# Another order for the last two units of a sliding-window attention and for wo's blocks

## The chip, the cores and the metric

The kernel runs on one core of a Trainium2 chip. The metric is the device time of one execution in microseconds (us), lower is better. Three runs of the kernel before took 217.32, 217.93 and 218.16 us; their median is 217.93 us.

## What is computed

One decoding step for two sequences (B = 2, one token each, D = 512), all in float32. `xn` is the layer norm of `x`. The output is `x + s * g`:

```python
q = (xn @ wq)                       # 32 heads of 128
k = k_cache[:, :, Sk - W:, :]       # the last W = 4096 of 32768 positions, 8 key heads
v = v_cache[:, :, Sk - W:, :]       # each key head serves 4 query heads
p = softmax(q k^T * 128 ** -0.5)
s = (p v).reshape(B, 1, 4096) @ wo  # wo is 4096 x 512: 8 MB
g = silu(gated_mlp(xn, w_in, w_sp, b_sp, w_out))
```

The windows of K and V are 2 x 8 x 4096 x 128 floats each, 32 MB apiece. With wq (8 MB), wo (8 MB) and the MLP's weights, 89.4 MB have to come from HBM, and each byte is used once.

## The kernel before

**Units and slots.** The 16 pairs of (sequence, key head) are handled two at a time, in eight units, 0 to 7. A unit's K and its V are one transfer of 4096 KB each. All large inputs go through a ring of four slots of 4096 KB (`ring`, line 105): the MLP's first weight, wq in two slots, then K and V in turn, and last wo in two slots, `wo0` and `wo1`. A transfer can be issued once the slot that it takes has been read for the last time. All of them are issued from SyncE's queue (SP) in program order.

**Steps of a unit.** VectorE turns K in eight pieces (`T:u.0` to `T:u.7`, line 373). For each half a of the unit TensorE multiplies the turned K with the queries (`shares`), ScalarE copies the product out of PSUM (`keep`), TensorE adds the shares up (`scores`), VectorE takes the maximum (`rowmax`). The maximum is shared (`mg`, `shmax`, `bias`), ScalarE takes the exponential (`exp`), VectorE turns the result (`probs_t`), and TensorE multiplies it with V (`pv`). The sum of the exponentials runs beside it (`lsum`, `shsum`, `weights`). At the end ScalarE moves the scaled result out of PSUM (`evac`), TensorE collects the heads (`col`), and VectorE adds them (`gather`).

**After a set of units.** The heads fall in three sets (`SETS`, line 360): the first holds half of wo's rows, the other two a quarter each. When the last unit of a set is gathered, TensorE spreads the heads (`spread:i`, line 490), VectorE places them as the stationary operand `oT` (`oT:i`, line 501), and the set's rows of wo can be multiplied. Set 0 is complete after unit 5, set 1 after unit 6, set 2 after unit 7.

**wo.** `wo0` holds set 0 (16 rows of 2 KB in each partition), `wo1` holds sets 1 and 2 (8 rows each). Line 515 cuts the loads: set 0 in two transfers of 2048 KB, set 1 in two of 1024 KB, set 2 in transfers of 1024, 512, 256 and 256 KB. So there are eight blocks. The steps `X` and `Y` (`wo_early`, line 523) multiply two rows each, for sets 0 and 1, into the PSUM tile `part`; twelve such steps make 24 multiplications. In code, `X:0.k` for k = 0 to 3 are block 0, for 4 to 7 block 1; `Y:0.0` and `Y:0.1` are block 2, `Y:0.2` and `Y:0.3` block 3.

**The end.** Lines 575 to 594 stand behind the order: ScalarE copies `part` to `parts`; TensorE multiplies blocks 4 to 7 (set 2) into `so`, with `parts` added after block 4; VectorE multiplies by the gate and adds x (`res`); SP stores 4 KB.

**Order.** The program order of all these steps is written out in the string `ORDER` (lines 27 to 52), and each engine's instructions are kept in it (`InOrder`, line 55). An engine works its own queue in that order: an instruction that waits holds up all that stand behind it on its engine, whatever they need themselves. Completion of transfers is signalled on eight semaphores that the framework gives to SP's transfers in turn, so a transfer also waits until the one eight places before it has landed.

Of the kernel before, what the change touches and what calls it, by code (L numbers as in the profile page):

```python
# [9 lines left out]
F32 = mybir.dt.float32  # L10
AF = mybir.ActivationFunctionType
# [3 lines left out]
P = 128  # L15
HQ, DH = 32, 128
G = 4
# [24 lines left out]
K:6 V:5 T:5.0 T:5.1 T:5.2 rowmax:4.1 mg:4 shmax:4 T:5.3 bias:4 shares:5.0 T:5.4 gather:3 exp:4.0 probs_t:4.0 T:5.5  # L42
T:5.6 exp:4.1 keep:5.0 pv:4.0 lsum:4 shsum:4 scores:5.0 T:5.7 shares:5.1 probs_t:4.1 pv:4.1 weights:4 keep:5.1
scores:5.1 evac:4 col:4 rowmax:5.0
K:7 V:6 T:6.0 rowmax:5.1 T:6.1 mg:5 T:6.2 shmax:5 T:6.3 T:6.4 bias:5 exp:5.0 exp:5.1 T:6.5 shares:6.0 probs_t:5.0
pv:5.0 lsum:5 T:6.6 keep:6.0 probs_t:5.1 T:6.7 shsum:5 scores:6.0 weights:5 shares:6.1 rowmax:6.0 pv:5.1
V:7 T:7.0 wo:0 keep:6.1 evac:5 scores:6.1 col:5 T:7.1 T:7.2 rowmax:6.1 mg:6 shmax:6 gather:5 spread:0 T:7.3 bias:6
T:7.4 T:7.5 shares:7.0 exp:6.0 probs_t:6.0 T:7.6 keep:7.0 pv:6.0 T:7.7 wo:1 exp:6.1 scores:7.0 shares:7.1 probs_t:6.1
keep:7.1 lsum:6 shsum:6 scores:7.1 rowmax:7.0 weights:6 pv:6.1 evac:6 rowmax:7.1 mg:7 shmax:7 col:6 oT:0 bias:7
gather:6 spread:1 exp:7.1 exp:7.0 probs_t:7.1 lsum:7 X:0.1 probs_t:7.0 X:0.3 X:0.2 shsum:7 weights:7 X:0.0 pv:7.0  # L50
pv:7.1 oT:1 evac:7 X:0.7 Y:0.1 X:0.4 X:0.5 col:7 Y:0.0 X:0.6 gather:7 spread:2 oT:2 Y:0.3 Y:0.2
"""


# [16 lines left out]
def kernel(  # L71
# [14 lines left out]
    pe, dve, act, sp = (InOrder(tc, e) for e in (nc.tensor, nc.vector, nc.scalar, nc.sync))  # L86
    B, _, D = x.shape
# [11 lines left out]
    DC = D // G  # L99
# [8 lines left out]
    sb = ctx.enter_context(tc.tile_pool(name="sb", bufs=2))  # L108
    ps = ctx.enter_context(tc.tile_pool(name="ps", bufs=1, space=bass.MemoryType.PSUM))

    def slot(name, *shape):
        return ring.tile([P, *shape], F32, tag="slot", name=name)

    def bank(name, *shape):
        return ps.tile([P, *shape], F32, tag="kt", name=name, bufs=2)
# [11 lines left out]
    for a in range(0, KT, 2):  # L127
        t = slot(f"wq{a}", 2, HQ * DH)
# [17 lines left out]
    def load(u, src, name):  # L146
        t = slot(f"{name}{u}", UJ, DH)
        b, v = divmod(u, HKV // 2)
        first = src[b, 2 * v, SK - W, :]
        of = bass.AP(tensor=src.tensor, offset=first.offset, ap=[[UJ * DH, P // 2], [SK * DH, 2], [1, UJ * DH]])  # L150
        sp.dma_start(t.rearrange("p j d -> p (j d)"), of)
        return t
# [17 lines left out]
    rowm = cst.tile([P, 32], F32, tag="rowm", name="rowm")  # L170
# [66 lines left out]
    for n in range(G):  # L237
        pz = bank(f"z{n}", 512)[:, :FC]
        for k in range(KT):
            pe.matmul(  # L240
                pz[32 * k : 32 * k + 32, :], xnT[:, k, :], win[:, k, n * FC : (n + 1) * FC],
                start=True, stop=True,
# [31 lines left out]
    u = cst.tile([P, 2, FT, B], F32, tag="u", name="u")  # L274
# [37 lines left out]
    for j in range(FT):  # L312
        for g in range(G):
            pe.matmul(
                y[32 * g : 32 * g + 32, :], hT[:, j, :], wout[:, j, g * DC : (g + 1) * DC],
                start=(j == 0), stop=(j == FT - 1),
# [20 lines left out]
    def place_queries():  # L337
        dve.tensor_tensor(
            free_ap(qb, 16, [[REP, G], [32, NP * G], [1, REP]]), free_ap(qa, 0, [[0, G], [REP, NP * G], [1, REP]]),
            free_ap(grpm, 0, [[1, G], [0, NP * G], [0, REP]]), op=ALU.mult,  # L340
        )

    gate = cst.tile([P, DC], F32, tag="gate", name="gate")

    def silu():
        dve.tensor_scalar(gate, ys, -1.0, 80.0, op0=ALU.mult, op1=ALU.min)
        act.activation(gate, gate, AF.Exp)
        dve.tensor_scalar_add(gate, gate, 1.0)
        dve.reciprocal(gate, gate)
        dve.tensor_mul(gate, gate, ys)  # L350
# [11 lines left out]
    for i, (kv, n, nj) in enumerate(SETS):  # L362
        o1 = cst.tile([P, B, 32], F32, tag=f"o1_{i}", name=f"o1_{i}")
        oT = cst.tile([P, nj, 32], F32, tag=f"oT_{i}", name=f"oT_{i}")
# [102 lines left out]
    col = {}  # L467
# [22 lines left out]
    def spread(i):  # L490
        o1, oT, nj = sets[f"oT{i}"]
        perm = {8: perm8, 16: perm16}[nj]
        nx = 32 // nj
        pts[i] = bank(f"oT_ps{i}", B, nj)
        for x in range(nx):
            pe.matmul(
                pts[i], perm[:, x].rearrange("p h a x -> p (h a x)"), o1[:, :, nj * x : nj * x + nj],
                start=(x == 0), stop=(x == nx - 1),
            )

    def place(i):
        dve.tensor_copy(sets[f"oT{i}"][1][:, :, 0 : 16 * B : 16], pts[i].rearrange("p b j -> p j b"))
# [6 lines left out]
    blocks = []  # L509

    def load_wo(n):
        t = slot(f"wo{n}", 16, D)
        a = 0
        for i in ((0,), (1, 2))[n]:
            for j, n in (((0, 8), (8, 8)), ((0, 4), (4, 4)), ((0, 4), (4, 2), (6, 1), (7, 1)))[i]:
                sp.dma_start(t[:, a : a + n, :], wo_s[i][:, j : j + n, :])
                blocks.append((t[:, a : a + n, :], sets[f"oT{i}"][1], j))
                a += n
# [4 lines left out]
    def wo_early(n, at):  # L523
        nonlocal done
        if done == 0:
            part.append(ps.tile([P, 512], F32, tag="s0", name="part"))
        t, oT, j = blocks[n]
        for a in range(at, at + 2):
            g = done % G
            pe.matmul(  # L530
                part[0][32 * g : 32 * g + 32, :], oT[:, j + a, :], t[:, a, :], start=(done < G), stop=(done >= EARLY - G)
            )
            done += 1

    part = []
    STEPS = dict(
        T=turn, rowmax=row_max, mg=spread_max, shmax=share_max, bias=bias, exp=probs, probs_t=probs_t, lsum=own_sum,
        shsum=share_sum, weights=weights, shares=shares, keep=keep, scores=scores, pv=pv, evac=evacuate, col=collect,
        gather=gather,
    )  # L540

    def step(name, u, a=()):
        if name == "q":
            place_queries()
        elif name == "silu":
            silu()
        elif name == "K":
            units[u].k = load(u, k_cache, "k")
        elif name == "V":
            units[u].v = load(u, v_cache, "v")  # L550
        elif name == "wo":
            load_wo(u)
        elif name == "spread":
            spread(u)
        elif name == "oT":
            place(u)
        elif name == "X":
            wo_early(a[0] // 4, 2 * (a[0] % 4))
        elif name == "Y":
            wo_early(2 + a[0] // 2, 2 * (a[0] % 2))  # L560
        else:
            STEPS[name](units[u], *a)

# [5 lines left out]
    for line in ORDER.strip().split("\n"):  # L569
        for name in line.split():  # L570
            name, at = name.split(":")
            u, _, a = at.partition(".")
            step(name, int(u), (int(a),) if a else ())

    parts = sb.tile([P, D], F32, tag="o", name="parts", bufs=1)
    act.activation(parts, part[0], AF.Copy)
    so = bank("so", DC)
    for n in range(4, len(blocks)):
        t, oT, j = blocks[n]
        for a in range(t.shape[1]):  # L580
            for g in range(G):
                pe.matmul(
                    so[32 * g : 32 * g + 32, :], oT[:, j + a, :], t[:, a, g * DC : (g + 1) * DC],
                    start=(j + a == 0), stop=(j + a == oT.shape[1] - 1),
                )
        if n == 4:
            for g in range(G):
                pe.matmul(
                    so[32 * g : 32 * g + 32, :], rowm, parts[:, g * DC : (g + 1) * DC], start=False, stop=False
                )  # L590
    res = cst.tile([P, DC], F32, tag="res", name="res")
    dve.tensor_mul(res, so, gate)
    dve.tensor_add(res, res, x4)
    sp.dma_start(bass.AP(tensor=out.tensor, offset=out.offset, ap=by_group), res[0 : P : P // (G * B), :])

# [27 lines left out]
```

## Time and profile before

| | before |
|---|---|
| runs shown (us) | 217.32, 217.93, 218.16 |
| profiled execution (us) | 217.48 |
| span from first to last instruction (us) | 215.7 |
| busy: PE, DVE, ACT (us) | 143.5, 126.3, 50.9 |
| mean granted TensorE clock | 0.826 |
| read from HBM | 89.40 MB, 414 GB/s over the span |

The profile is that of one execution; its own time of 217.48 us is its span of 215.7 us and 1.8 us around it. In its rows PE is TensorE's matmuls, PEld the loading of their stationary operand, DVE VectorE, ACT ScalarE and SPq SyncE's queue. Each operation stands as out<-in by the names of the tiles: `kts<-k` is `T`, `sh` is `shares`, `s` is `scores`, `p` is `exp`, `pT` is `probs_t`, `acc` is `pv`, `o<-acc` is `evac`, `col` is `col`, `o<-col` is `gather`, `oT_ps` is `spread`, `oT` is the placing, `part` is X and Y, and `so` is the last product. All lines appear as L65, since a helper there issues every instruction, so the tiles tell them apart. A float32 matmul leaves two records: the 24 multiplications of X and Y stand as 48.

### The profile page before, as it was taken

What the parts mean: (1) busy time and instruction counts of PE and PEld (TensorE: products, weight loads), DVE (VectorE), ACT (ScalarE), POOL (GpSimd) and SP (SyncE); (2) the same over time, 40 slices, a digit from 0 to 9 for tenths busy, and PEclk for the clock granted to TensorE, in tenths of its full rate; (3) what the DMA queues carried; (4) which work ended last, traced back from release to release, by engine and by line L of the source; (5) the groups of instructions that cost most, each with busy time, mean ns of one, the idle gap of its engine ahead of it and who ended that gap; (6) DMA issues with size and microseconds to landing.
All of it is one profiled execution on the core that took longest, in us unless ns stands there. A gap on an engine that the chain in (4) does not pass through costs nothing.

```text
span 215.7 us, 2477 instructions
## 1 busy us (share of the span) xinstructions
PE 143.5 (67%) x972; PEld 51.6 (24%) x972; DVE 126.3 (59%) x217; ACT 50.9 (24%) x128; POOL 5.2 (2%) x19
## 2 busy tenths in 40 slices
PE   0179694722864895954990796389168939975993
PEld 0128521300111232312220221122112322221342
DVE  2511212259598989849918972993698199534001
ACT  4111203200114236023330603142032305242020
POOL 8000000000000000000000000000000000000000
PEclk9998578785589699995796589579955985997999
DMA  6999999999999999999999999999999999999990
GB/s 256 426 438 444 407 428 468 395 463 407 462 413 441 431 425 444 419 448 407 456 413 456 419 441 431 419 444 422 450 409 462 407 450 419 441 401 428 419 376 23
DMA packets 4219, 89.56 MB, mean 415 GB/s; under 512 B 478, under 2 KB 494, under 8 KB 880
## 3 DMA queue, kind: packets, MB, share of 16 engines
q1 hardware_dynamic: 4188, 89.40, 96.6%
q8 instruction: 8, 0.13, 0.2%
q10 hardware_dynamic: 20, 0.01, 0.0%
q14 instruction: 3, 0.02, 0.0%
HBM read 89.40 MB, written 0.00 MB: 414 GB/s over the span
## 4 chain that ended last, share of the span: by engine, by line
DMA 57%; PE 20%; DVE 17%; ACT 4%; issue 1%; ACTq 0%
DMA k<-in_A_k_cache_dram 40%; DMA wo<-in_A_wo_dram 12%; DVE kts L65 11%; PE acc L65 7%; DMA win<-in_B_w_in_dram 5%; PE sh L65 5%; PE part L65 4%; ACT p L65 3%; PE s L65 3%; DVE pT L65 2%; DVE m L65 1%; PE so L65 1%; DVE gate L65 1%; DVE nb L65 1%; ACT ss L65 1%
## 5 line engine op out<-in xcount | busy, mean ns | idle before, releaser
L65 DVE STREAM_TRANSPOSE kts<-k 128x1024 f32<-128x1024 f32 x64 | 75.7, 1219 | 25.7 <-DMA k<-in_A_k_cache_dram 25.7
L65 PE MATMUL sh<-kts,qb 128*32 128x512 f32 x256 | 42.9, 793 | 12.5 <-DVE kts L65 9.0
L65 PE MATMUL acc<-v,pT 128*32 128x512 f32 x256 | 36.4, 676 | 6.9 <-DVE pT L65 4.0
L65 ACT ACTIVATE p<-s,nb 128x512 f32<-128x512 f32 x32 | 22.5, 730 | 38.6 <-DVE nb L65 38.6
L65 ACT ACTIVATE ss<-sh 128x512 f32<-128x512 f32 x16 | 9.6, 599 | 61.4 <-PE sh L65 61.4
L65 DVE STREAM_TRANSPOSE pT<-p 128x1024 f32<-128x1024 f32 x16 | 19.6, 1226 | 2.5 <-ACT p L65 2.5
L65 PE MATMUL s<-ss,sums 128*128 128x512 f32 x32 | 18.8, 671 | 2.1 <-ACT ss L65 2.1
L65 PE MATMUL mo<-mg,joint 128*128 128x16 f32 x16 | 4.2, 338 | 23.6 <-DVE mg L65 23.6
L65 PEld LDWEIGHTS acc<-v,pT 128*32 128x32 f32 x256 | 11.4, 143 | 32.6 <-issue 21.8
L65 PEld LDWEIGHTS sh<-kts,qb 128*32 128x32 f32 x256 | 8.8, 128 | 35.1 <-issue 31.1
L65 DVE TENSOR_REDUCE m<-s 128x1 f32<-128x512 f32 x16 | 10.8, 678 | 5.9 <-PE s L65 5.8
L65 PE MATMUL q_ps<-wq,xnT 128*32 128x512 f32 x64 | 11.0, 820 | 4.6 <-DMA wq<-in_A_wq_dram 4.6
L65 ACT ACTIVATE o<-acc,wd 128x128 f32<-128x128 f32 x32 | 9.1, 367 | 19.5 <-PE acc L65 19.5
L65 PE MATMUL part<-wo,oT 128*32 128x512 f32 x48 | 9.5, 709 | 2.4 <-DMA wo<-in_A_wo_dram 2.4
L65 PEld LDWEIGHTS mo<-mg,joint 128*128 128x128 f32 x16 | 3.3, 261 | 26.8 <-DVE mg L65 24.2
L65 PE MATMUL z<-win,xnT 128*32 128x448 f32 x32 | 5.2, 814 | 3.9 <-DMA win<-in_B_w_in_dram 3.9
L65 PEld LDWEIGHTS s<-ss,sums 128*128 128x128 f32 x32 | 5.0, 197 | 10.4 <-issue 7.4
L65 PE MATMUL zT_ps<-rowm,z 128*128 128x2 f32 x28 | 6.6, 370 | 0.0
L65 PEld LDWEIGHTS zT_ps<-rowm,z 128*128 128x128 f32 x28 | 6.5, 325 | 0.0
L65 ACT ACTIVATION_READ_ACCUMULATOR p<-s,nb 128x1 f32 x32 | 6.4, 200 | 0.0
L65 ACT ACT_TABLE_LOAD x4 | 5.1, 1283 | 2.6 <-POOL hT L164 2.6
L65 PE MATMUL xnT_ps<-ident,xn 2*128 2x2 f32 x4 | 0.6, 253 | 7.5 <-DVE xn L65 7.5
(108 smaller groups left out, 71.4 us busy)
## 6 DMA issues: line engine op xcount, KB each, us to landing
k<-in_A_k_cache_dram SPq DMA_DIRECT2D x8, 4096.0 KB, 23.8
v<-in_A_v_cache_dram SPq DMA_DIRECT2D x8, 4096.0 KB, 29.8
wq<-in_A_wq_dram SPq DMA_DIRECT2D x1, 4096.0 KB, 24.3
wq<-in_A_wq_dram SPq DMA_DIRECT2D x2, 2048.0 KB, 29.4
wo<-in_A_wo_dram SPq DMA_DIRECT2D x2, 2048.0 KB
win<-in_B_w_in_dram SPq DMA_DIRECT2D x1, 3584.0 KB
wo<-in_A_wo_dram SPq DMA_DIRECT2D x3, 1024.0 KB, 24.3
wout<-in_B_w_out_dram SPq DMA_DIRECT2D x1, 1792.0 KB, 15.0
```

Source lines behind the costliest of these rows:

```text
L65: return self.tc.keep_in_program_order(call(*args, **kwargs))
```

## The change

The string `ORDER` is another one from unit 6 on, set 0 and set 1 of wo come in one transfer each (4096 and 2048 KB, where there were two and two), and what stood behind the order is now part of it, as steps `Z` (one block of set 2 each), `parts` (the copy of `part`) and `pz` (adding it). `X:0.k` is now rows 2k and 2k + 1 of block 0, and `Y:0.k` the same of block 1: the same rows of wo as before. The loads of K and V keep their places in SP's queue. With three transfers fewer ahead of it, the store gets another of the eight semaphores.

Three things in the order are different. In units 5 to 7 the exponentials of both halves stand closer together and the sum's steps elsewhere among VectorE's turns. `pv:7.0` and `pv:7.1` now stand ahead of every X step, where X:0.1, X:0.3, X:0.2 and X:0.0 stood ahead of them. And spread:0 stands after unit 7's exponentials instead of in unit 7's turns.

```diff
-K:7 V:6 T:6.0 rowmax:5.1 T:6.1 mg:5 T:6.2 shmax:5 T:6.3 T:6.4 bias:5 exp:5.0 exp:5.1 T:6.5 shares:6.0 probs_t:5.0
-pv:5.0 lsum:5 T:6.6 keep:6.0 probs_t:5.1 T:6.7 shsum:5 scores:6.0 weights:5 shares:6.1 rowmax:6.0 pv:5.1
-V:7 T:7.0 wo:0 keep:6.1 evac:5 scores:6.1 col:5 T:7.1 T:7.2 rowmax:6.1 mg:6 shmax:6 gather:5 spread:0 T:7.3 bias:6
-T:7.4 T:7.5 shares:7.0 exp:6.0 probs_t:6.0 T:7.6 keep:7.0 pv:6.0 T:7.7 wo:1 exp:6.1 scores:7.0 shares:7.1 probs_t:6.1
-keep:7.1 lsum:6 shsum:6 scores:7.1 rowmax:7.0 weights:6 pv:6.1 evac:6 rowmax:7.1 mg:7 shmax:7 col:6 oT:0 bias:7
-gather:6 spread:1 exp:7.1 exp:7.0 probs_t:7.1 lsum:7 X:0.1 probs_t:7.0 X:0.3 X:0.2 shsum:7 weights:7 X:0.0 pv:7.0
-pv:7.1 oT:1 evac:7 X:0.7 Y:0.1 X:0.4 X:0.5 col:7 Y:0.0 X:0.6 gather:7 spread:2 oT:2 Y:0.3 Y:0.2
+K:7 V:6 T:6.0 rowmax:5.1 mg:5 T:6.1 T:6.2 shmax:5 bias:5 T:6.3 exp:5.0 T:6.4 exp:5.1 T:6.5 probs_t:5.0 shares:6.0
+keep:6.0 lsum:5 shsum:5 scores:6.0 probs_t:5.1 T:6.6 T:6.7 rowmax:6.0 pv:5.0 weights:5 shares:6.1 keep:6.1 pv:5.1
+V:7 T:7.0 wo:0 scores:6.1 rowmax:6.1 T:7.1 T:7.2 mg:6 T:7.3 shmax:6 bias:6 T:7.4 evac:5 col:5 exp:6.0 exp:6.1 T:7.5
+probs_t:6.0 T:7.6 T:7.7 wo:1 lsum:6 shares:7.0 keep:7.0 pv:6.0 scores:7.0 shares:7.1 rowmax:7.0 keep:7.1 shsum:6
+scores:7.1 probs_t:6.1 weights:6 rowmax:7.1 mg:7 pv:6.1 evac:6 shmax:7 gather:5 col:6 bias:7 exp:7.0 gather:6 exp:7.1
+probs_t:7.0 spread:0 probs_t:7.1 lsum:7 spread:1 pv:7.0 shsum:7 oT:0 weights:7 pv:7.1 X:0.6 X:0.0 oT:1 X:0.2 X:0.4
+evac:7 X:0.3 col:7 X:0.7 gather:7 spread:2 X:0.5 Y:0.1 Y:0.0 Y:0.3 X:0.1 Y:0.2 parts:0 oT:2 Z:0 Z:1 pz:0 Z:2 Z:3
...
-            for j, n in (((0, 8), (8, 8)), ((0, 4), (4, 4)), ((0, 4), (4, 2), (6, 1), (7, 1)))[i]:
+            for j, n in (((0, 16),), ((0, 8),), ((0, 4), (4, 2), (6, 1), (7, 1)))[i]:
...
+    def copy_parts():
+        parts.append(sb.tile([P, D], F32, tag="o", name="parts", bufs=1))
+        act.activation(parts[0], part[0], AF.Copy)
+
+    def wo_last(n):
+        if n == 0:
+            so.append(bank("so", DC))
+        t, oT, j = blocks[2 + n]
+        for a in range(t.shape[1]):
+            for g in range(G):
+                pe.matmul(
+                    so[0][32 * g : 32 * g + 32, :], oT[:, j + a, :], t[:, a, g * DC : (g + 1) * DC],
+                    start=(j + a == 0), stop=(j + a == oT.shape[1] - 1),
+                )
+
+    def add_parts():
+        for g in range(G):
+            pe.matmul(
+                so[0][32 * g : 32 * g + 32, :], rowm, parts[0][:, g * DC : (g + 1) * DC], start=False, stop=False
+            )
...
-            wo_early(a[0] // 4, 2 * (a[0] % 4))
+            wo_early(0, 2 * a[0])
         elif name == "Y":
-            wo_early(2 + a[0] // 2, 2 * (a[0] % 2))
+            wo_early(1, 2 * a[0])
+        elif name == "Z":
+            wo_last(u)
+        elif name == "parts":
+            copy_parts()
+        elif name == "pz":
+            add_parts()
...
-    parts = sb.tile([P, D], F32, tag="o", name="parts", bufs=1)
-    act.activation(parts, part[0], AF.Copy)
-    so = bank("so", DC)
-    for n in range(4, len(blocks)):
...
-    dve.tensor_mul(res, so, gate)
+    dve.tensor_mul(res, so[0], gate)
```

More of the change, by code (lines that the diff above doesn't have):

```diff
@@ L535 @@
     part = []
+    def copy_parts():
[16 more added lines that the diff above has]
+            )
+    parts, so = [], []
     STEPS = dict(
@@ L573 @@
             step(name, int(u), (int(a),) if a else ())
-    parts = sb.tile([P, D], F32, tag="o", name="parts", bufs=1)
-    act.activation(parts, part[0], AF.Copy)
-    so = bank("so", DC)
-    for n in range(4, len(blocks)):
[L579 to L590, printed above, removed]
     res = cst.tile([P, DC], F32, tag="res", name="res")
-    dve.tensor_mul(res, so, gate)
+    dve.tensor_mul(res, so[0], gate)
     dve.tensor_add(res, res, x4)
```

## The prediction, made before the changed kernel was run

> **What bounds the kernel now.** I read the page's queue line first, then the chain of waits in order of time, SP's rows, and last the tail by stretches.
>
> ```profile
> q1 hardware_dynamic: 4188, 89.40, 96.6%
> ```
> ```profile
> 89.05 25.00 DMA k<-in_A_k_cache_dram
> ...
> 126.12 26.71 DMA k<-in_A_k_cache_dram
> ...
> 171.43 25.47 DMA wo<-in_A_wo_dram
> ...
> 197.03 3.56 PE part L65 x12
> ...
> 210.10 2.12 PE so L65 x72
> ```
> ```profile
> 166.15 0.54 SPq L65 DMA_DIRECT2D v<-in_A_v_cache_dram  x1
> ```
> ```profile
> 171.43 0.81 SPq L65 DMA_DIRECT2D wo<-in_A_wo_dram  x2
> ```
> ```profile
> 184.01 2.23 SPq L65 DMA_DIRECT2D wo<-in_A_wo_dram  x5
> ```
> ```profile
> SPq L65 <- DVE res L65: 15.9, 1, 15.9
> SPq L65 <- DMA v<-in_A_v_cache_dram: 5.8, 1, 5.8
> SPq L65 <- DMA wo<-in_A_wo_dram: 4.5, 1, 4.5
> ```
> ```profile
> 192.07 0.33 SPq L65 DMA_DIRECT2D wo<-in_A_wo_dram  x1
> 212.89 0.69 SPq L65 DMA_DIRECT2D out_dram<-res  x1
> ```
>
> The transfers keep the 16 DMA engines at 96.6% of the span: one stream without a break. Its pace: K4 landed at 89.05 + 25.00 = 114.05 and K6 at 126.12 + 26.71 = 152.83, four transfers of 4096 KB later, so 9.70 us each. SP could issue the last piece of wo only at 192.07, when V7 had landed. The first half of set 0 landed at 171.43 + 25.47 = 196.90, so 2048 KB took 4.83 us. The other 6 MB of wo, at 9.70 us for 4 MB, end at 196.90 + 14.55 = 211.45.
>
> The stream never waits for a slot here: V7 was issued at 166.15, wo0 at 171.43, wo1 from 184.01 on, each with 16 to 20 us of earlier transfers still under way.
>
> The tail:
>
> ```profile
> 196.98:200.39 3.41, 3.36 (x12) 0.65 (x12) 0.00 (x0) 0.00 (x0) 0.00 (x0) 0.50 1.00 428
> 200.39:203.80 3.41, 3.41 (x32) 1.62 (x34) 0.48 (x3) 0.00 (x0) 0.00 (x0) 1.00 0.98 416
> 203.80:207.21 3.41, 3.41 (x40) 1.46 (x36) 0.00 (x0) 1.14 (x4) 0.00 (x0) 1.00 1.02 423
> ```
> ```profile
> 211.00:211.20 0.20, 0.20 (x12) 0.20 (x13) 0.00 (x0) 0.00 (x0) 0.00 (x0) 1.00 0.13 51
> 211.20:211.40 0.20, 0.20 (x16) 0.20 (x12) 0.00 (x0) 0.00 (x0) 0.00 (x0) 1.00 0.00 0
> ```
> ```profile
>   DMA wo<-in_A_wo_dram: 2.4, 1
> ```
> ```profile
> 210.23 0.60 ACT L65 ACTIVATE parts<-part 128x512 f32<-128x512 f32 x1 [3.67 <-PE part L65]
> 210.88 0.43 PE L65 MATMUL so<-parts,rowm 128*32 128x128 f32 x8
> 211.12 1.06 PE L65 MATMUL so<-wo,oT 128*32 128x128 f32 x32
> 212.24 0.29 DVE L65 TENSOR_TENSOR res<-so,gate 128x128 f32<-128x128 f32 x1 [2.85 <-PE so L65]
> ```
>
> The columns of the stretches are: length, busy time (and count) of PE, PEld, DVE, ACT and POOL, then granted clock, DMA share and GB/s. From 197.03 to 212.18 PE has no pause. It waits for wo exactly once, 2.4 us before 197.03: X:0.1 holds `pv:7.0` up in PE's queue until wo's first half is there. That wait costs twice, as the clock is 0.50 in the next stretch. The last bytes of wo leave the engines by 211.2, and my sum of landings says 211.45. So PE and the stream arrive together, PE perhaps a little later. **Two bounds of nearly the same height** make the end; moving PE's work can gain only what lies between them.
>
> **The change, part by part.**
>
> *Issues of V7, wo0 and wo1.* V7 waits for T:6.7, wo0 for `pv:5.1`, wo1 for T:7.7. VectorE does the same instructions between T:6.0 and T:6.7 as before, and up to T:7.7 one less (the gather of unit 5 comes later); TensorE does the same ones before `pv:5.1`. So each moves by less than 1 us, and the stream hides all of it; that cover of 16 us or more would have to go first. Cost: nothing. *Fewer transfers.* SP issues three less, and the last of wo need not wait for V7's landing, but the bytes ahead of it last until about 201.7 anyway: nothing. For size, 4 MB as two halves cost 2 x 4.83 = 9.66 us, as one 9.70: between -0.1 and +0.1 us for both sets; I take 0. *The store's semaphore.* Its wait on `wo` ended 15.9 us ahead of `res`: nothing.
>
> *Unit 7's tail.* Rows for its pieces:
>
> ```profile
> 189.50 1.96 PE L65 MATMUL acc<-v,pT 128*32 128x512 f32 x16
> ...
> 192.54 0.74 ACT L65 ACTIVATE p<-s,nb 128x512 f32<-128x512 f32 x1
> 192.72 0.16 PEld L65 LDWEIGHTS col<-o,selw 128*32 128x32 f32 x8 [1.03 <-ACT o L65]
> 192.72 0.43 PE L65 MATMUL col<-o,selw 128*32 128x128 f32 x8 [0.93 <-ACT o L65]
> ...
> 193.55 1.06 PE L65 MATMUL oT_ps<-o,perm 128*128 128x16 f32 x8 [0.41 <-DVE o L65]
> ```
> ```profile
> 205.15 0.16 PEld L65 LDWEIGHTS part<-wo,oT 128*32 128x32 f32 x4 [0.27 <-issue]
> 205.41 1.14 ACT L65 ACTIVATE o<-acc,wd 128x128 f32<-128x128 f32 x4 [9.98 <-PE acc L65]
> 205.58 0.12 PEld L65 LDWEIGHTS part<-wo,oT 128*32 128x32 f32 x2 [0.27 <-issue]
> ```
> ```profile
> 207.30 0.29 DVE L65 TENSOR_REDUCE o<-col 128x32 f32<-128x128 f32 x1 [5.84 <-PE col L65]
> ```
>
> One X or Y step is one such round of PEld, 205.58 - 205.15 = 0.43 us at full clock. Unit 7 reaches its exponentials at 192.5 as now, since `pv:6.1`, `evac:6` and `shmax:7` keep their order. PE then does spread:0 and spread:1 (2 x 1.06, from 193.2 to 195.3), `pv:7.0` and `pv:7.1` (1.96 each, with `shsum` 0.4) to **199.7**, against 205 now. `evac:7` (1.14) ends by 201. PE then waits for all of set 0: 192.07 + 9.66 = 201.73, start 201.9. Queued behind this wait are `col:7`, spread:2 and the rest of wo. Five X steps (2.15) and `col:7` (0.43) end at 204.5; `gather` (0.29), spread:2 (1.06) and the last X at 206.5. Set 1 lands at 201.73 + 4.85 = 206.6; its four Y steps and X:0.1 last 2.15 and 0.6 for the last to drain, to 209.45; `parts` (0.60) to 210.1. Z:0 finds its block at 209.0, Z:1 at 210.2, Z:2 at 210.8, Z:3 at 211.45 by the stream's pace. Z:3 is one row, like the `parts` group of 0.43, and starts about 0.13 after landing (196.90 to 197.03): 211.58 + 0.43 = 212.0, against 212.18. So the tail gains between 0 (if the last block lands when PE got to it now) and 0.2 us: I take 0.1. PE's new slack does not help: what is late next is the stream itself.
>
> *Sum.* 217.48 - 0.1 = 217.4 us for an execution like the profiled one, which lies 0.45 below the median shown. I cannot tell whether that 0.45 is PE's tail, which would go, or the stream, which would stay; half of it gives **217.6 us**.
>
> *A rule against the change.* These rows have the clock after pauses:
>
> ```profile
> 173.08:176.49 3.41, 0.00 (x0) 0.00 (x0) 3.38 (x5) 0.00 (x0) 0.00 (x0) 1.00 0.91 394
> 176.50:179.90 3.40, 3.19 (x18) 1.85 (x22) 3.37 (x7) 1.51 (x4) 0.00 (x0) 0.50 1.00 434
> ```
> ```profile
> 180.07:183.48 3.41, 3.05 (x19) 0.47 (x12) 3.41 (x4) 1.57 (x4) 0.00 (x0) 0.52 1.02 442
> ...
> 190.15:193.56 3.41, 2.06 (x26) 0.62 (x15) 1.14 (x6) 2.04 (x7) 0.00 (x0) 1.00 0.95 408
> 193.56:196.97 3.41, 1.06 (x8) 0.96 (x8) 2.55 (x3) 1.87 (x6) 0.00 (x0) 1.00 0.98 418
> ```
>
> A stretch of 3.41 us with PE busy for 1.06 us was followed by one at 0.50; after 2.06 us the clock stayed at 1.00. The new pause, 199.7 to 201.9, would be cut by this run's border at 200.39 into 0.7 and 1.5 us; the stretch behind the border is busy for 1.9 us, and keeps the clock. The Trainium skill, "TensorE: Matmul & The Clock Gate", section "What's actually happening", has the clock halved after an idle window of about 3.4 us, in windows that run free of the kernel's start. The trace is harsher: 1.06 us of work did not save it. Where the borders fall otherwise, the pause lies in one stretch and halves the next.
>
> **The rivals.**
>
> 1. *The clock halves behind the wait for set 0 (slower).* One stretch at 0.50 loses 3.41 / 2 = 1.7 us of PE's work. The Y steps would then drain at 210.5, having their data long before; `parts` ends at 211.15, `pz`, Z:2 and Z:3 end near 212.1: no loss yet. From the second half-speed stretch on every us counts: 1.5 us more, **219.0**. For it: 176.50 to 183.3 shows two in a row. Against: PE has work without pause from 201.9 on, and 196.98 to 200.39, full of work, was a single one.
>
> 2. *The larger transfers are slower.* V6's last bytes came by 182.0, V7's at 192.07, as the next row and SP's show: 10.06 us for one 4096 KB transfer. Should wo's 6 MB in larger pieces go at that pace: 1.5 x (10.06 - 9.70) = 0.54, **218.1**. Nothing but noise speaks for it.
>
> ```profile
> 182.15 2.48 PE L65 MATMUL acc<-v,pT 128*32 128x512 f32 x16 [0.36 <-DMA v<-in_A_v_cache_dram]
> ```
>
> 3. *The runs above the profiled one were PE's tail.* It has no slack now and gets 1.5 us. Then runs fall to the stream's floor, 217.48 - 0.2 - 0.1 (size) = **217.2**, 0.3% under the median, 0.45% under the slowest run.
>
> 4. *Each transfer has a fixed cost that shows.* The lone store needs 0.69 to issue and 1.0 us of waiting:
>
> ```profile
> SPq L618 <- DMA out_dram<-res: 1.0, 1, 1.0
> ```
>
> Three transfers less by 1.7 us each would give 217.4 - 5.1 = **212.3**. Against: halves and wholes go at the same pace, 9.66 and 9.70. The Trainium skill, "DMA: Bandwidth & Descriptors", section "Anatomy of one DMA — SWDGE (gpsimd) path", gives 2.0 us a transfer, which would make it 6 us; the trace agrees for a lone transfer, and not in a full queue.
>
> **Chances.** The forecast 0.64, rival 1 0.15, rival 2 0.07, rival 3 0.12, rival 4 0.02. About 0.5% is what a measurement of this kernel can tell from no change. Slower by more: 0.13 of rival 1 and 0.02 of rival 2, 0.15. Faster by more: rival 4 and 0.06 of rival 3, 0.08. Between: 0.77. The range goes from 216.9, 0.3 below rival 3 for its unknown sizes, to rival 1's 219.0; rival 4 and the worse half of rival 1 stay out.
>
> **What would show it.** Right: the chain ends in DMA wo, then `so`; PE waits for wo several times, first for about 2 us near 199.7 and at the last blocks; `pv:7.1` ends before 200; the last `so` still ends near 212.0. Wrong: PE busy without pause up to its last `so` at a clock of 0.50 (rival 1), or a stream that ends before 210.5 or after 212.

## The result, and the profile after

The changed kernel took 217.0 us (median of 20 runs), the kernel before 217.56 us in 20 runs beside it. The ratio is 0.9973, with a 95% interval from 0.9962 to 0.9985: 0.27% faster, inside the 0.5% that was called no change, and inside the range, near its lower end.

One slip first: of wo there are two transfers fewer, six in place of eight, and not three as the texts above have it. Nothing else in them hangs on that but rival 4, whose price would be 3.4 us instead of 5.1.

The profiled execution of the changed kernel took 217.3 us, with a span of 215.4. It is one of its slowest: its 20 spans go from 215.0 to 215.4 us, median 215.1. The runs' times also hold 1.74 to 2.96 us around the span, in kernels of both orders alike; so below the spans are compared as well.

The end of its chain of waits, in order of time (start, length, what):

```profile
185.48 26.11 DMA wo<-in_A_wo_dram
211.59 0.04 issue
211.64 0.47 PE so L65 x8
212.11 0.02 issue
212.13 0.30 DVE res L65
212.43 0.02 issue
212.46 0.29 DVE res L65
```

Before, 15.2 us of PE's work stood here without a break. Now the last piece of wo lands at 211.59, and one row's product follows. What waited for wo, from the view of that tile, shows it too:

```profile
  DMA wo<-in_A_wo_dram: 1.7, 3
```

Three waits where there was one. The timeline has them (idle time and what ended it in brackets):

```profile
194.93 2.68 PE L65 MATMUL acc<-v,pT 128*32 128x512 f32 x16 [0.76 <-DVE pT L65]
...
198.05 2.59 PE L65 MATMUL acc<-v,pT 128*32 128x512 f32 x16
...
201.60 2.34 PE L65 MATMUL part<-wo,oT 128*32 128x512 f32 x18 [0.96 <-DMA wo<-in_A_wo_dram]
...
206.00 3.22 PE L65 MATMUL part<-wo,oT 128*32 128x512 f32 x24
...
210.42 0.38 PEld L65 LDWEIGHTS so<-wo,oT 128*32 128x32 f32 x16 [0.32 <-DMA wo<-in_A_wo_dram]
...
211.64 0.16 PEld L65 LDWEIGHTS so<-wo,oT 128*32 128x32 f32 x8 [0.40 <-DMA wo<-in_A_wo_dram]
212.13 0.29 DVE L65 TENSOR_TENSOR res<-so,gate 128x128 f32<-128x128 f32 x1 [5.78 <-PE so L65]
```

The two `pv:7` steps run ahead of the wait for wo and end at 200.6, against 205. `res` starts at 212.13, against 212.24: 0.11 us of gain by the tail. The last piece landed at 211.59 in the trace of before as well, so here the two can be compared directly. The stretches around that show the clock:

```profile
192.61:196.02 3.41, 2.65 (x28) 1.98 (x28) 2.55 (x3) 2.36 (x8) 0.00 (x0) 1.00 0.96 413
196.02:199.43 3.41, 3.41 (x19) 0.92 (x14) 0.87 (x6) 0.00 (x0) 0.00 (x0) 0.50 0.88 380
```

PE was at half clock for most of `pv:7`, which I had not expected. So its pause behind `pv:7.1` is only 0.96 us, not 2.2.

The rest of the gain stands behind the store. SP's own waits in the last microseconds, of the changed kernel:

```profile
SPq L631 <- DMA out_dram<-res: 0.7, 1, 0.7
```

It was 1.0 us before. SP ends the program with a check of each semaphore, and each check takes a turn. From the trace, SP's instructions from the store on, before and after (start, length, semaphores that it waits for; the store's is marked):

```
before                              after
212.89 0.691 store (on 101*)        212.78 0.695 store (on 110*)
213.64 0.017 102                    213.53 0.017 102
213.70 0.965 103, 101*              213.59 0.028 103, 101
214.69 0.027 104, 100               213.65 0.028 104, 100
214.76 0.028 107, 105               213.71 0.028 107, 105
214.82 0.028 109, 108               213.77 0.028 109, 108
214.88 0.028 110, 106               214.54 0.028 110*, 106
214.95 0.013 99                     214.61 0.013 99
```

Before, the store's landing was waited for in the second check, and five steps of 0.06 us followed it, 214.66 to 214.95. Now it stands in the last pair: the others are done while the store is under way.

### The profile page after: what moved, and what is told of

Read it like the earlier page. It is cut to its first block, busy times and chain, and to the rows that moved or that the text cites. A ratio compares the mean times of both kernels' runs of the same rounds, so it can differ in the third digit from the quotient of the medians.

```text
span 215.4 us, 2476 instructions
## 1 busy us (share of the span) xinstructions
PE 139.0 (65%) x972; PEld 50.7 (24%) x972; DVE 125.7 (58%) x217; ACT 51.1 (24%) x128; POOL 5.2 (2%) x19
## 4 chain that ended last, share of the span: by engine, by line
DMA 68%; DVE 23%; ACT 3%; PE 2%; issue 1%; SPq 1%
DMA k<-in_A_k_cache_dram 51%; DVE kts L65 18%; DMA wo<-in_A_wo_dram 12%; DMA win<-in_B_w_in_dram 5%; DVE pT L65 2%; ACT p L65 2%; PE sh L65 2%; DVE m L65 1%; DVE gate L65 1%; SPq L65 1%; DVE nb L65 1%; PE s L65 1%; DVE qb L65 1%; ACT ss L65 0%; DVE res L65 0%
## 5 line engine op out<-in xcount | busy, mean ns | idle before, releaser
L65 PE MATMUL sh<-kts,qb 128*32 128x512 f32 x256 | 43.4, 803 | 15.5 <-DVE kts L65 12.0
L65 PE MATMUL acc<-v,pT 128*32 128x512 f32 x256 | 35.1, 665 | 6.5 <-DMA v<-in_A_v_cache_dram 4.3
L65 PE MATMUL s<-ss,sums 128*128 128x512 f32 x32 | 17.9, 642 | 2.5 <-ACT ss L65 2.5
L65 PEld LDWEIGHTS acc<-v,pT 128*32 128x32 f32 x256 | 10.6, 142 | 30.9 <-issue 21.7
L65 PE MATMUL q_ps<-wq,xnT 128*32 128x512 f32 x64 | 9.0, 689 | 5.2 <-DMA wq<-in_A_wq_dram 5.2
L65 PE MATMUL part<-wo,oT 128*32 128x512 f32 x48 | 6.2, 595 | 1.0 <-DMA wo<-in_A_wo_dram 1.0
L65 DVE TENSOR_REDUCE o<-col 128x32 f32<-128x128 f32 x6 | 1.6, 270 | 6.9 <-PE col L65 6.9
```

Source lines behind the costliest of these rows:

```text
L65: return self.tc.keep_in_program_order(call(*args, **kwargs))
```

## The experiments

The theory: the end is set by the later of two things, the stream of transfers and PE's tail; PE was late in part of the runs, by how the clock's stretches fell; and the closing checks add their part. The rivals: the larger transfers end the stream sooner; or another part of the new order did it. All ratios are to the kernel before on the same chip. In the 87 runs of it that stand behind the ratios from before_again on, its spans go from 215.3 to 216.7 us, with medians of 215.7 to 215.8 by chip.

The last column takes the one profiled execution of each kernel apart: when the last piece of wo landed, how long after that `res` started, and how long after that the span ended. For the first profile of the kernel before it is 211.59 + 0.66 + 3.45.

| kernel | median us | ratio, 95% interval | spans: least, median, most | profiled: landing, to `res`, to the end |
|---|---|---|---|---|
| changed | 217.0 | 0.9973 (0.9962 to 0.9985) | 215.0, 215.1, 215.4 | 211.59 + 0.54 + 3.23 |
| before_again | 218.0 | 1.0004 (0.9985 to 1.0024) | 215.3, 215.95, 216.9 | 211.21 + 0.62 + 3.43 |
| order_alone | 217.32 | 0.9976 (0.9960 to 0.9992) | 215.3, 215.45, 215.7 | 211.56 + 0.54 + 3.45 |
| transfers_alone | 222.85 | 1.0222 (1.0199 to 1.0245) | 219.9, 221.1, 221.6 | 211.48 + 5.23 + 3.22 |
| pv_first | 217.36 | 0.9982 (0.9966 to 0.9998) | 215.3, 215.5, 215.9 | 211.29 + 0.54 + 3.43 |
| pause_filled | 217.36 | 0.9997 (0.9968 to 1.0025) | 215.3, 215.4, 217.8 | 211.40 + 2.84 + 3.43 |
| before_more2 | 218.88 | 1.0051 (1.0033 to 1.0070) | 216.5, 217.1, 217.7 | 211.37 + 2.67 + 3.43 |
| after_more2 | 216.95 | 0.9969 (0.9952 to 0.9986) | 214.9, 215.15, 215.7 | 211.50 + 0.54 + 3.22 |
| after_more7 | 218.8 | 1.0042 (1.0010 to 1.0074) | 215.3, 216.95, 218.5 | 211.31 + 3.98 + 3.21 |
| order_store_last | 217.51 | 0.9987 (0.9970 to 1.0003) | 215.2, 215.55, 216.2 | 211.94 + 0.80 + 3.22 |
| after_store_early | 217.46 | 0.9984 (0.9967 to 1.0001) | 215.2, 215.45, 215.8 | 211.46 + 0.54 + 3.43 |
| x_in_product | 216.74 | 0.9950 (0.9930 to 0.9971) | 214.6, 214.95, 215.2 | 211.55 + 0.54 + 2.89 |

Three things stand in that column. The last landing lies anywhere from 211.2 to 211.9 us, and the two profiles of the kernel before alone differ in it by 0.4 us. `res` follows it after 0.54 us in all six kernels whose PE is ready for the last piece, and later where PE is late. And the rest takes 3.43 to 3.45 us where the store has the semaphore of before, 3.21 to 3.23 where it has a later one (x_in_product, at 2.89, also leaves out a step).

### The kernel before once more

> The kernel before once more, to see span and clock of each of its runs. It took 217.22 to 218.42 us in 20 runs, half of them above 217.55; the changed kernel's spans are 215.0 to 215.4 us in all 20. Theory (two bounds: the stream of transfers and PE's tail, PE late in some runs): the spans spread too, from about 215.3 to 216.5 us. Rival (the spread lies around the span, as in the changed kernel's two runs at 217.94 and 218.16): all spans within 0.4 us.

No edit. Its 12 spans spread over 1.6 us, those of the changed kernel over 0.4. So the spread of before lies inside the span, as the theory says. Whether it is the clock's is another question. The profiled execution is a short one, 215.3 against the 215.7 of the first profile, and the clock is halved in nearly the same stretch in both (196.87 to 200.28 here). What differs is the stream: the first half of set 0 landed at 196.48 instead of 196.90, and the 15.2 us of PE's work began that much sooner.

```profile
170.13 26.34 DMA wo<-in_A_wo_dram
196.48 0.14 issue
196.61 3.42 PE part L65 x12
...
209.68 2.12 PE so L65 x72
```

So a tail without slack also hands on every change of that landing. No profile shows one of its longer executions (216 us or more), so how much of the spread is the clock's is not shown by this kernel; before_more2 below shows it for one execution of nearly the same code.

### The order without the transfers

The diff to the changed kernel (and the numbers of the blocks in X, Y and Z to match):

```diff
-            for j, n in (((0, 16),), ((0, 8),), ((0, 4), (4, 2), (6, 1), (7, 1)))[i]:
+            for j, n in (((0, 8), (8, 8)), ((0, 4), (4, 4)), ((0, 4), (4, 2), (6, 1), (7, 1)))[i]:
```

> The changed order, with wo in the eight transfers of before; the store falls back to its old semaphore. Theory (the order alone brings the gain, the size of the transfers nothing): 217.0 us, ratio 0.997, as the whole change. Rival (the larger transfers end the stream sooner): 217.4 us, ratio 0.999 to 1.000.

The spans shrink to 0.4 us of spread, median 215.45: 0.35 to 0.5 us under before (215.8 in the runs on the same chip, 215.95 in before_again), and 0.35 above the changed kernel. The ratio is the theory's; the time of 217.32 lies nearer the rival's. Does the stream end later with eight transfers? The end of its chain:

```profile
191.97 19.60 DMA wo<-in_A_wo_dram
211.56 0.04 issue
211.61 0.47 PE so L65 x8
212.08 0.02 issue
212.10 0.30 DVE res L65
```

It lands at 211.56, the changed kernel's at 211.59. Over all profiles the median landing is 211.40 in the seven with eight transfers (211.21 to 211.94) and 211.49 in the six with six (211.31 to 211.59). So the transfers' size brings nothing that can be seen at the landing; the order takes away PE's late runs; and 0.35 us is left to explain.

### The transfers without the order

```diff
-            for j, n in (((0, 8), (8, 8)), ((0, 4), (4, 4)), ((0, 4), (4, 2), (6, 1), (7, 1)))[i]:
+            for j, n in (((0, 16),), ((0, 8),), ((0, 4), (4, 2), (6, 1), (7, 1)))[i]:
```

> The order of before, with sets 0 and 1 of wo in one transfer each. X:0.1, ahead of pv:7.0 in PE's queue, then waits for the whole of set 0, to 201.6 us in place of 196.9. Theory (PE's tail of 15.2 us starts with that wait and has no slack): 4.7 us later, less 1.7 us if the clock stays whole: 220 to 222.5 us. Rival (larger transfers help by themselves): 217.0 us.

222.85 us, slower by 2.2%, a little above what was expected; in its trace the clock was at 0.50 from 194.29 to 204.53. Its timeline:

```profile
201.81 3.24 PE L65 MATMUL part<-wo,oT 128*32 128x512 f32 x12 [5.99 <-DMA wo<-in_A_wo_dram]
...
205.79 3.56 PE L65 MATMUL acc<-v,pT 128*32 128x512 f32 x28
```

X:0.1 waits for the whole of set 0 and holds `pv:7` up with it. So the larger transfers are harmless only behind the new order.

### Unit 7's pv ahead of X, and nothing else

```diff
-gather:6 spread:1 exp:7.1 exp:7.0 probs_t:7.1 lsum:7 X:0.1 probs_t:7.0 X:0.3 X:0.2 shsum:7 weights:7 X:0.0 pv:7.0
-pv:7.1 oT:1 evac:7 X:0.7 Y:0.1 X:0.4 X:0.5 col:7 Y:0.0 X:0.6 gather:7 spread:2 oT:2 Y:0.3 Y:0.2
+gather:6 spread:1 exp:7.0 exp:7.1 probs_t:7.0 pv:7.0 probs_t:7.1 lsum:7 shsum:7 weights:7 pv:7.1 X:0.1 X:0.3
+X:0.2 X:0.0 oT:1 evac:7 X:0.7 Y:0.1 X:0.4 X:0.5 col:7 Y:0.0 X:0.6 gather:7 spread:2 oT:2 Y:0.3 Y:0.2
```

> The kernel before with one thing of the new order: unit 7's exponentials and turns in the order 0, 1, and both pv:7 steps ahead of the four X steps that stood before them. Transfers, and the rest of the order, as before. Theory (the pause of PE ahead of pv:7 is what makes its tail late): 217.0 us, ratio 0.997, and a narrow spread. Rival (the earlier exponentials of units 5 and 6, the late spread:0 or the transfers bring it): 217.5 us, with the spread of before.

Median span 215.5, as order_alone: this one exchange (with unit 7's halves in the order 0, 1) is what the order brings, but for a slightly wider spread. PE starts `pv:7` when unit 7 is ready, and now has time to wait for wo:

```profile
195.21 1.96 PE L65 MATMUL acc<-v,pT 128*32 128x512 f32 x16 [0.76 <-DVE pT L65]
...
201.48 1.05 PE L65 MATMUL part<-wo,oT 128*32 128x512 f32 x4 [0.41 <-DMA wo<-in_A_wo_dram]
204.01 1.48 PE L65 MATMUL part<-wo,oT 128*32 128x512 f32 x10 [1.47 <-DMA wo<-in_A_wo_dram]
...
211.33 0.43 PE L65 MATMUL so<-wo,oT 128*32 128x128 f32 x8 [0.18 <-DMA wo<-in_A_wo_dram]
```

### PE's pause filled

```diff
+    def more(n):
+        t = ps.tile([P, 512], F32, tag="s1", name="more")
+        for i in range(2 * n):
+            g = i % G
+            pe.matmul(
+                t[32 * g : 32 * g + 32, :], selw[:, 0:32], units[7].v[:, 0:4, :].rearrange("p j d -> p (j d)"),
+                start=True, stop=True,
+            )
...
-... lsum:7 X:0.1 probs_t:7.0 ...
+... lsum:7 more:5 X:0.1 probs_t:7.0 ...
```

> The kernel before with ten matmuls of no use (five steps of 0.43 us, shaped like X steps, into an unused bank) in PE's pause ahead of X:0.1, from about 194.6 to 196.9 us. They delay nothing. Theory (the pause halves the clock behind it, and that makes PE's tail late in part of the runs): granted clock 1.00 from 196.97 us on, time 217.1 us, narrow spread. Rival (the clock has nothing to do with it): 217.5 us with the spread of before.

Two kinds of runs: nine spans from 215.3 to 215.6, the stream's floor, and three at 217.7 and 217.8. The profile is of one of the latter:

```profile
190.66:194.07 3.41, 2.06 (x25) 0.89 (x17) 0.89 (x5) 2.32 (x8) 0.00 (x0) 1.00 0.98 418
194.07:197.48 3.41, 3.41 (x19) 1.85 (x23) 2.56 (x3) 1.58 (x6) 0.00 (x0) 0.50 1.01 432
197.48:200.90 3.42, 3.42 (x18) 0.75 (x12) 0.00 (x0) 0.00 (x0) 0.00 (x0) 0.50 0.97 412
```

There the clock had already halved at 194.07, so the filling itself ran at half speed, from 195.4 to about 200, and pushed everything behind it back. Over all runs the ratio decides nothing, and the narrow spread that the theory foretold did not come. But the two kinds belong to the same code, and the clock of the one that was profiled is halved over two stretches; in it `res` starts 2.84 us behind the landing. That the nine others had a whole clock is not shown.

### More work for PE, before and after

```diff
-pv:7.1 oT:1 evac:7 ...                 (before)
+pv:7.1 more:2 oT:1 evac:7 ...
-... weights:7 pv:7.1 X:0.6 ...         (changed)
+... weights:7 pv:7.1 more:2 X:0.6 ...  (and more:7 in another kernel)
```

> The kernel before with 0.86 us of matmuls of no use (two steps, results unread) behind pv:7.1. Theory (no slack in PE's tail): 0.4 to 0.9 us slower than before, 218.0 to 218.4 us. Rival (the stream alone is the bound): no change, 217.5 us.

> The changed kernel with the same 0.86 us of matmuls of no use behind pv:7.1. Theory (its PE tail has slack, some 2 us in its profile): no change, 217.0 us, ratio to before 0.997. Rival (PE's tail is still a bound): 217.5 to 217.9 us.

> The changed kernel with 3.0 us (seven steps) of matmuls of no use behind pv:7.1. In its profile PE pauses behind pv:7.1 for 0.96, 0.95, 0.3 and 0.4 us, 2.6 us in all. Theory (the slack is the sum of the pauses): 0.4 to 1.2 us slower than the changed kernel, 217.4 to 218.2 us, with the slower clock not in play. Rival (the stream hides all): 217.0 us.

The same 0.86 us costs the kernel before 1.1 us (0.51%; I had expected 0.4 to 0.9), and even its least span rises from 215.3 to 216.5. It costs the changed kernel nothing: in its profile `res` still starts 0.54 us behind the landing. That is the plainest sign that PE's tail was a bound and is none now. In the profile of before_more2 the clock was at 0.50 over two stretches:

```profile
195.93:199.34 3.41, 2.57 (x12) 0.65 (x12) 0.44 (x1) 0.00 (x0) 0.00 (x0) 0.50 1.01 432
199.34:202.76 3.42, 3.42 (x18) 1.13 (x18) 0.48 (x3) 0.00 (x0) 0.00 (x0) 0.50 0.96 407
```

Up to `pv:7.1` this kernel is the kernel before, whose clock was whole again from 200.39 on. From the first half of set 0 to the end of `so` its PE takes 17.25 us (196.77 to 214.02 in its chain), 2.06 more than the 15.19 of before (197.03 to 212.22): 0.86 for the work added, and 1.2 left. The clock stood at 0.50 for 5.99 us of this tail instead of 3.36; half of the difference is 1.3 us, about what is left. So where the stretches fall does move this tail.

With 3.0 us more the changed kernel rises by 1.85 us at the median, more than the 0.4 to 1.2 expected, and spreads from 215.3 to 218.5: in the best runs nearly all of it is hidden. The profile is of the longest run: there the clock was at 0.50 from 173.15 to 186.80 and again from 197.04 to 200.46, and `pv:7.0` began at 197.04, where the changed kernel's began at 194.93. What the other runs' clock did is not shown. So the slack lies between 0.9 and 3 us, and seems to change from run to run.

### The store's semaphore

The framework gives the eight semaphores out in turn, so halving some early transfers moves the store's:

```diff
-        sp.dma_start(t.rearrange("p j d -> p (j d)"), of)
+        flat = t.rearrange("p j d -> p (j d)")
+        if name == "v" and u in (1, 2):   # order_store_last: (1, 2, 3, 4, 5, 6), on order_alone
+            half = UJ * DH // 2
+            for h in range(2):
+                of = bass.AP(
+                    tensor=src.tensor, offset=first.offset + h * half,
+                    ap=[[UJ * DH, P // 2], [SK * DH, 2], [1, half]],
+                )
+                sp.dma_start(flat[:, h * half : (h + 1) * half], of)
+            return t
+        sp.dma_start(flat, of)
```

> The changed kernel with V1 and V2 in two halves each, which counts the store's semaphore on by two, to the one it had before. wo's transfers are the changed ones. Theory (closing checks): spans about 215.4 us, 0.25 to 0.3 longer than the changed kernel's 215.1. Rival (the larger transfers save it): 215.1 us.

> The changed order with wo in the eight transfers of before, as in order_alone (spans 215.3 to 215.7 us, median 215.45), and V1 to V6 in two halves each. That counts the store's semaphore on by six, to the one that SP checks last at the end. Theory (SP's closing checks behind the store's landing are what the semaphore saves, four of 0.06 us): spans about 215.15 us, as the whole change (median 215.1). Rival (the larger transfers of wo save the 0.3 us): 215.45 us.

after_store_early has all of the change but the semaphore, and loses 0.35 us: median span 215.45, as order_alone. The profiles show 0.2 of it behind `res`, 3.43 against 3.23; the rest may be the spread of the landings. From its trace, the store's landing is again waited for in the second check (213.44, for 0.95 us), with five steps behind it:

```profile
SPq L641 <- DMA out_dram<-res: 1.0, 1, 1.0
```

The rival's 215.1 did not come. The other kernel missed: 215.55, where 215.15 was expected. Its checks are as short as the changed kernel's: from the store's landing at 215.13 to the last check's end 0.05 us, where order_alone has 0.29. But in its profile the last piece landed only at 211.94, 0.35 us later than the changed kernel's, and its PE was late again: `pv:7.1` ends at 198.7 and the pause lasts 3.13 us, nearly all of it in one stretch:

```profile
196.74 1.95 PE L65 MATMUL acc<-v,pT 128*32 128x512 f32 x16
201.83 2.94 PE L65 MATMUL part<-wo,oT 128*32 128x512 f32 x16 [3.13 <-DMA wo<-in_A_wo_dram]
```

```profile
199.19:202.60 3.41, 0.77 (x8) 0.34 (x12) 0.00 (x0) 0.77 (x3) 0.00 (x0) 1.00 0.95 404
202.60:206.02 3.42, 3.42 (x24) 1.42 (x18) 0.00 (x0) 0.00 (x0) 0.00 (x0) 0.50 1.01 424
```

`res` then starts 0.80 us behind the landing, where 0.54 would do, so PE's lateness costs 0.26 us. Behind `res` the span takes 3.22 us, where order_alone takes 3.45: the shorter checks do save 0.2 us with eight transfers too, and in this run the late landing and the late PE hide it. Why its spans reach 216.2, where order_alone's end at 215.7, stays open.

### x brought in ahead of the last landing

If all behind the last landing counts, the addition of x behind the product can go ahead of it. x divided by the gate is worked out in unit 1's turns and joins the product on PE, where there is slack. Where the gate is exactly 0, this version leaves x out: the product is multiplied by 0 after x has joined it.

```diff
+        dve.tensor_scalar(xg, gate, 0.0, 0.0, op0=ALU.is_equal, op1=ALU.add)
+        dve.tensor_add(xg, xg, gate)
+        dve.reciprocal(xg, xg)
+        dve.tensor_mul(xg, xg, x4)
...
                 so[0][32 * g : 32 * g + 32, :], rowm, parts[0][:, g * DC : (g + 1) * DC], start=False, stop=False
             )
+            pe.matmul(
+                so[0][32 * g : 32 * g + 32, :], ident[:, 32 * g : 32 * g + 32], xg, start=False, stop=False
+            )
...
-    dve.tensor_add(res, res, x4)
```

> The changed kernel with x brought in through the last product: x divided by the gate is computed early on VectorE, one more matmul per group adds it to so ahead of Z:2, and the addition of x behind the product, 0.33 us from res to res, is left out. Theory (what stands behind the last landing counts in full, PE has slack ahead of it): spans about 214.8 us, 216.65 us in all. Rival (the matmuls more, or the VectorE steps more in unit 1's turns, cost as much): 215.1 us.

```profile
211.00 0.44 PE L65 MATMUL so<-xg,ident 128*32 128x128 f32 x8
...
212.09 0.29 DVE L65 TENSOR_TENSOR res<-so,gate 128x128 f32<-128x128 f32 x1 [5.48 <-PE so L65]
212.41 0.69 SPq L65 DMA_DIRECT2D out_dram<-res  x1
```

The store leaves 0.32 us behind the start of `res`, not 0.65. 216.74 us, ratio 0.9950 (0.9930 to 0.9971); the spans' median fell by 0.15 of the expected 0.33 against the changed kernel's, which was not measured beside it. In the profiles the whole 0.33 is there: from the start of `res` to the end 2.89 us, against 3.23. The landings, which vary by more, stand between the two. The two intervals overlap, so its lead over the changed kernel is likely, not certain; it was 0.5% faster than the kernel before.

## Why the prediction was right, point by point

**Two bounds of nearly the same height: right.** pv_first lowers the one and shows the other just below it; the two kernels with 0.86 us more show which of them was the higher.

**Issues of V7, wo0 and wo1 hidden: right.** V7's landing, when set 0's transfer begins, is at 191.6 to 192.1 in all profiles. That each issue would move by less than 1 us did not hold for wo0, issued at 169.62 instead of 171.43. But in the second profile of the kernel before it stands at 170.13, and the stream hid it all.

**Fewer and larger transfers, 0 within 0.1 us: right.** The last landing is at 211.56 with eight and at 211.59 with six, and the medians of all profiles are 211.40 and 211.49. As single landings spread by up to 0.7 us, this is as fine as the profiles can tell.

**The store's semaphore, nothing: this step failed.** I weighed only what the store waits for before it is issued, not who waits for the store. The row that gave the wait before `res` was read rightly, but the store's own landing, 1.0 us of waiting in a row shown under rival 4, was put at no cost to the end. By the closing rows the change of place saves 0.24 us, by the thirteen profiles 0.2 behind `res`; after_store_early measures 0.35 with it against without.

**The tail's gain, 0.1 us: right** for the profiled executions (0.11; that their last pieces landed at the same time was luck), **and too small for the median.** I could not tell whether the median's 0.45 us above the profiled run was PE or the stream, and took half. Most of that 0.45 was neither: it came of a median of three runs, and in 20 runs the median is 217.56, only 0.08 above the profiled run. So the forecast of 217.6, set against 217.56, came to no gain at all, and 217.0 falls into the range only because its lower end had been set 0.3 under rival 3. What the order gives is more than 0.1: order_alone and pv_first lower the median span by 0.3 to 0.5. So rival 3 (217.2) came nearest. From 217.56, 0.3 to 0.5 for the order and 0.2 for the semaphore would have given 216.9 to 217.1, and 217.0 was measured.

**The path there was not quite as foretold.** I had the clock whole during `pv:7` and a pause of 2.2 us behind it; it was halved, and the pause 0.96 us. The end was the same, as the slack took it up.

**Rival 1** is no phantom: it shows in order_store_last, where the clock is halved behind a pause of 3.13 us, and PE is 0.26 us late at the last piece. The changed kernel's 20 spans differ by no more than 0.4 us, so there it cost little or nothing. The Trainium skill, "TensorE: Matmul & The Clock Gate", section "What's actually happening", says that the windows run free of the kernel's start. The borders of the stretches agree with that: one lies at 196.98 in the profile of before, at 195.93 in before_more2's and at 197.48 in pause_filled's.

**Rival 2** did not show. **Rival 4** did not either: two transfers fewer moved the landing by 0.03 us the other way, where 3.4 us would have been its price. The 2.0 us a transfer quoted beside it from the Trainium skill stand in a section on the "SWDGE (gpsimd) path"; SP issues the transfers here, so they do not price these.

## What to carry to other kernels

Where two bounds end together, ask which of them varies from run to run: taking from the varying one what holds it up lowers the median though the best run stays. In an engine's queue, put what is ready ahead of what waits for a late transfer, above all on TensorE, whose pause may be paid for a second time by its clock. And follow the chain to the program's last instruction: what the end waits for, in which order, counts as any other step does.

## What the runs showed of the hardware that was not expected

PE's busy time in a stretch does not tell the clock of the next. 2.34 and 2.38 us of 3.41 kept it whole, and 2.65 and 2.06 halved it, though 2.06 had kept it in the kernel before:

```profile
189.70:193.10 3.40, 2.34 (x26) 0.77 (x18) 1.19 (x6) 1.75 (x7) 0.00 (x0) 1.00 0.96 410
193.11:196.52 3.41, 2.38 (x20) 1.50 (x24) 2.71 (x4) 2.14 (x8) 0.00 (x0) 1.00 1.02 437
196.52:199.94 3.42, 3.42 (x34) 1.22 (x30) 0.53 (x5) 0.47 (x2) 0.00 (x0) 1.00 1.00 429
```

These are of pv_first; the 2.65 is the changed kernel's row above, the 2.06 that of pause_filled. The changed kernel's stretch holds spread:0 and spread:1, matmuls of 16 and 32 columns with long loads of the stationary operand. That such short matmuls fill PE's rows but count little for the clock would fit, and no run tried it.

The traces can be counted, though: each matmul record as partitions x columns x elements, put into the stretch in which it starts. By that count the 2.06 us that kept the clock held 21.8 million, and the 2.06 us that did not 16.0. Of the 462 stretches at a whole clock in the thirteen traces, all 104 with up to 16 million were followed by 0.50, whatever PE's busy time (0 to 3.41 us), and all 297 with over 29.5 million by 1.00. The 61 between went both ways, and the changed kernel's stretch is one of them (29.4, halved, where pv_first's 27.3 kept it). So the work done tells more than the time busy, but why this one stretch halved stays open.
